# One fused attention, MoE and gated-MLP kernel on one core: the first group's x parts taken straight from PSUM, and one recombination started at another distance

## The chip, the cores and the metric

The kernel runs on one NeuronCore of one Trainium2 chip. The metric is the device time of one execution in microseconds; the median of several runs is compared. TensorE is called PE here, VectorE DVE, ScalarE ACT, GpSimd POOL and SyncE SP, as in the profile.

## What is computed

The reference chains three stages. Attention works within chunks of 64 tokens; its output becomes x, 2304 tokens by 512. A mixture of four experts (MoE) follows, then one gated layer with a clip (MoE2). All is float32.

```python
scores = scale * np.matmul(q_c, k_c.transpose(0, 1, 2, 4, 3))     # chunks of 64, 8 heads of 64
attn = softmax(scores); out = np.matmul(attn, v_c)
x = out.transpose(0, 2, 1, 3).reshape(B * S, H * D)               # 2304 x 512
for e in range(4):
    h = np.maximum(x @ w1[e], 0.0)                                # 512 -> 1024
    y += p[:, e:e + 1] * (h @ w2[e])                              # 1024 -> 512
h = y @ w_in                                                      # 512 -> 2048
g = h * np.clip(h + 3.0, 0.0, 6.0) / 6.0
return g @ w_out                                                  # 2048 -> 512
```

## The kernel before

**Arithmetic.** PE multiplies in a format with a shortened mantissa (fp32r). Each float32 operand is therefore split in a high part (a rounding copy) and a low part (what is left over), and each product is done in three: high by high, high by low, low by high (the list `HL`). Most large products also go through a scheme of the Strassen kind with seven products in place of eight (P1 to P7 for the first weight matrix, M1 to M7 for the second); its sums and differences run on DVE, ACT and POOL.

**Order of work.** The 2304 tokens make three sets of 768; a set's tokens lie in two halves of N = 384, even and odd tokens. Phase 0 is the MoE, phase 1 is MoE2; a unit is one set with one group of 512 hidden columns. `h_pair` (its products stand at L1003) computes h in seven products; `y_unit` (L1344), `y_sevens` (L1181), `y_turned` (L1240) and `y_turned_plain` (L1292) compute y. The very first group, that is phase 0, set 0, group 0, is done in plain products (`h_plain`, L1062) and in three units of 128 even and 128 odd tokens, so that PE can begin before all of the set's attention is done.

**The first set's attention** is six items, each of 256 tokens and four heads (two pairs of heads): items 0 and 1 are tokens 0 to 255, 2 and 3 the next 256, 4 and 5 the last. An item (`Item.place`) loads q and k, sorts even from odd tokens on ACT, DVE or POOL (L484), transposes both on PE (L494), copies them out of PSUM (L497), multiplies scores (L512), takes the maximum and subtracts it on DVE (L536, L556) and exponentiates on ACT (L560), or leaves the subtraction to ACT's bias (`on_act`, L544); sums and divides (L564 to L570); transposes the weights on PE (L574), copies them out (L577) and multiplies by v (L583). `end` then copies the result from PSUM to `xs` (L606), and `build_plain` makes the high part of x from `xs` on ACT (L761) and the low part on DVE (L764). The weights of the first group are split by `split_w` into a high part on ACT (L789) and a low part on DVE or POOL (L791).

**Who orders it.** All instructions are given to a planner (`Plan`): each has an engine, an estimated duration, a due time, buffers that it takes and buffers that it uses. The planner plays the program through with these estimates, picks on each engine the ready instruction with the earliest due time, and writes the instructions down in that order; on the chip each engine runs its own list in order and waits at semaphores. So a change of a due time or of an estimate can move any instruction. While PE would have nothing to do before 24 us, the planner puts in a filler: a matmul of the identity (L324), whose result nobody reads. Numbers at the head of the file (`ITEMS`, `LEAD`, `LOADS` and others) shift due times.

**PSUM** has eight banks under three names: four "h", three "y", one "a"; one "y" belongs to the filler while it is needed.

**MoE2's recombination.** For sets 0 and 1, `y_turned` adds the seven products of three groups into SBUF sums (L1251). Before the last group, `recombine_turned` turns them into the four quarters of the result with seven additions for each of two halves b (L1265): half 0 on POOL, half 1 on DVE, the latter due `RGAP` later. The gate of MoE2 is at L1094 (ACT), L1095 (DVE), L1117 (high part) and L1119 (low part); L1013 are the additions of the seven-product scheme behind h, L710 and L720 the high and low parts of x for the next set, L726 its differences.

## Time and profile before

| | |
|---|---|
| median of 3 runs | 1167.76 us (1167.74 to 1168.73) |
| the profiled execution, its time | 1167.89 us |
| the profiled execution, its span | 1166.0 us |
| PE busy | 1156.4 us, 99% |
| DVE, ACT, POOL busy | 751.2, 493.0, 537.0 us (64%, 42%, 46%) |
| chain that ended last, by engine | PE 97%, DVE 2%, the rest 1% |
| HBM traffic | 220.76 MB read, 83.36 MB written, 261 GB/s over the span |

The span runs from the first to the last instruction of the core. PE is busy nearly all of it, so the three other engines matter where PE waits for them, and the first 60 us, in which the attention of the first set is made, are read by themselves.

### The profile page before, as it was taken

How to read it: one execution, taken by the hardware profiler on the slowest of the kernel's cores; microseconds unless marked ns; L12 is line 12 of the kernel's file. 1: busy time of each engine (PE TensorE's matmuls, PEld its weight loads, DVE VectorE, ACT ScalarE, POOL GpSimd, SP SyncE). 2: the span in 40 equal slices, each digit the busy share in tenths (PEclk: the TensorE clock that was granted, in tenths of full speed). 3: DMA queues.
4: the chain of work that ended last, by engine and by line, in shares of the span. 5: the costliest groups of instructions: out<-in, count | busy, mean ns of one | idle time of the engine just before them, and what ended most of it. 6: DMA issues, size and time to landing. Idle time of an engine off the chain costs nothing.

```text
span 1166.0 us, 20404 instructions
## 1 busy us (share of the span) xinstructions
PE 1156.4 (99%) x7286; PEld 1070.7 (92%) x7286; DVE 751.2 (64%) x1473; ACT 493.0 (42%) x1182; POOL 537.0 (46%) x464
## 2 busy tenths in 40 slices
PE   8999999999999999999999999999999999999998
PEld 8899888889999988889999998999999999999997
DVE  5656555558756656569646556568479947884685
ACT  6754444535253343425342333233533454435432
POOL 3577655665341252536442534343445244614470
PEclk9999999999999999999999999999999999999999
DMA  9579888767869989874878787987795789669751
GB/s 243 221 255 335 287 299 273 265 239 233 250 214 309 319 299 299 280 269 134 269 291 306 266 296 251 308 345 263 283 302 198 201 333 292 211 197 353 253 182 55
DMA packets 175910, 305.49 MB, mean 262 GB/s; under 512 B 95168, under 2 KB 101568, under 8 KB 175808
## 3 DMA queue, kind: packets, MB, share of 16 engines
q1 hardware_dynamic: 174064, 302.48, 76.5%
q10 hardware_dynamic: 1744, 1.70, 0.4%
q8 instruction: 58, 0.95, 0.3%
q14 instruction: 44, 0.36, 0.1%
HBM read 220.76 MB, written 83.36 MB: 261 GB/s over the span
## 4 chain that ended last, share of the span: by engine, by line
PE 97%; DVE 2%; issue 1%; ACT 0%; POOL 0%; DVEq 0%; POOLq 0%; ACTq 0%
PE h L1003 43%; PE y L1344 35%; PE y L1240 4%; PE h L1240 2%; PE y L1181 2%; PE y L1292 2%; PE h L1062 2%; PE h L1181 1%; PE a L1240 1%; PE h L1292 1%; PE a L574 1%; PE a L1181 1%; PE y L324 1%; PE h L583 0%; PE y L494 0%
## 5 line engine op out<-in xcount | busy, mean ns | idle before, releaser
L1003 PE MATMUL h<-x,wh 128*128 128x384 f32 x2940 | 520.0, 335 | 1.6 <-DVE t L1095 1.6
L1003 PEld LDWEIGHTS h<-x,wh 128*128 128x128 f32 x2940 | 510.1, 188 | 4.9 <-DVE t L1095 2.6
L1344 PE MATMUL y<-wy,gt 128*128 128x512 f32 x1800 | 421.7, 392 | 0.1
L1344 PEld LDWEIGHTS y<-wy,gt 128*128 128x128 f32 x1800 | 335.0, 188 | 70.2 <-DVE acc L1381 1.4
L1381 DVE SCALAR_TENSOR_TENSOR acc<-y,pn,acc 128x512 f32<-128x512 f32 x126 | 89.0, 749 | 135.0 <-PE y L1344 135.0
L1086 ACT ACTIVATE gt<-h 128x384 fp32r<-128x384 f32 (+1 forms) x150 | 69.1, 489 | 115.7 <-DVE h L1013 114.7
L1013 DVE TENSOR_TENSOR h<-h,c 128x384 f32<-128x384 f32 x152 | 85.2, 563 | 35.4 <-PE h L1003 34.7
L1119 POOL TENSOR_TENSOR gt<-t,gt 128x384 fp32r<-128x384 f32 x54 | 54.5, 1016 | 114.3 <-ACT gt L1117 113.7
L939 POOL TENSOR_TENSOR w<-w,rh 128x512 f32<-128x512 f32 x28 | 37.6, 1343 | 137.1 <-DVE rh L936 83.2
L1020 ACT COPY p<-h 128x384 f32<-128x384 f32 x70 | 33.6, 480 | 152.8 <-PE h L1003 152.7
L1013 DVE TENSOR_TENSOR c<-h,p 128x384 f32<-128x384 f32 x70 | 38.9, 556 | 82.4 <-PE h L1003 73.1
L1087 DVE SCALAR_TENSOR_TENSOR gt<-h,gt 128x384 fp32r<-128x384 f32 (+1 forms) x150 | 76.5, 541 | 21.7 <-ACT gt L1086 20.7
L791 POOL TENSOR_TENSOR wp<-t,wp 128x512 fp32r<-128x512 f32 x36 | 47.3, 1314 | 50.4 <-ACT wp L789 50.4
L1094 ACT ACTIVATE t<-h,half 128x384 f32<-128x384 f32 x84 | 46.1, 581 | 49.6 <-DVE h L1013 45.5
L791 POOL TENSOR_TENSOR wy<-t,wy 128x512 fp32r<-128x512 f32 x32 | 41.1, 1293 | 43.5 <-ACT wy L789 43.5
L791 POOL TENSOR_TENSOR wp<-rh,wp 128x512 fp32r<-128x512 f32 x24 | 31.2, 1298 | 61.5 <-ACT wp L789 38.4
L1013 DVE TENSOR_TENSOR c<-h,c 128x384 f32<-128x384 f32 x70 | 38.8, 554 | 18.2 <-PE h L1003 17.6
L720 POOL TENSOR_TENSOR x<-xs,x 128x384 fp32r<-128x384 f32 x16 | 18.5, 1170 | 67.4 <-ACT x L710 67.3
L1117 ACT CAST gt<-t 128x384 fp32r<-128x384 f32 x66 | 33.0, 516 | 27.6 <-POOL t L1126 19.1
L710 ACT CAST x<-xs 128x768 fp32r<-128x768 f32 x33 | 27.1, 835 | 40.9 <-DVE xs L726 33.4
L791 POOL TENSOR_TENSOR wh<-t,wh 128x512 fp32r<-128x512 f32 x28 | 36.9, 1333 | 13.7 <-ACT wh L789 13.7
L789 ACT CAST wp<-t 128x512 fp32r<-128x512 f32 x36 | 22.6, 629 | 41.1 <-DMA k<-wp 18.5
(266 smaller groups left out, 1590.1 us busy)
## 6 DMA issues: line engine op xcount, KB each, us to landing
wh<-k SPq DMA_DIRECT2D x182, 512.0 KB, 6.2
wy<-k SPq DMA_DIRECT2D x104, 512.0 KB, 5.4
k<-wp SPq DMA_DIRECT2D x60, 512.0 KB, 5.2
k<-wh SPq DMA_DIRECT2D x49, 512.0 KB, 4.4
k<-wy SPq DMA_DIRECT2D x32, 512.0 KB, 4.5
wp<-k SPq DMA_DIRECT2D x18, 512.0 KB, 6.5
t<-in_moe_w_dram SPq DMA_DIRECT2D x32, 256.0 KB, 4.9
rh<-in_moe_w_dram SPq DMA_DIRECT2D x8, 1024.0 KB, 7.7
```

Of the source, the lines that this page charges most:

```text
L791: return op(eng, gps(512) if eng == "POOL" else dve(512), lambda: e.tensor_tensor(out=view(b.t[:, 1]), in0=read(), in1=raw(view(b.t[:, 0]) ...
L939: nc.gpsimd.tensor_tensor(out=low(), in0=low(), in1=dst(), op=ALU.mult)
L1003: nc.tensor.matmul(acc.t[:, :n], W.t[:, a, k_ * 256 + pr_ * P:k_ * 256 + (pr_ + 1) * P], X.t[:, b, k_, cs], start=new and first, stop=last ...
L1013: add = lambda out, x, y: (lambda: nc.vector.tensor_tensor(out=out(), in0=x(), in1=y(), op=ALU.add))
L1086: hi = op("ACT", act(n), lambda: nc.scalar.activation(hi_(), src(), AF.Relu), due, after, [G], bufs)
L1087: lo = op("DVE", dve(n), lambda: nc.vector.scalar_tensor_tensor(out=lo_(), in0=src(), scalar=0.0, in1=raw(hi_()), op0=ALU.max, op1=ALU.sub ...
L1094: x = op("ACT", act(n), lambda: nc.scalar.activation(r_(), src(), AF.Relu, bias=half, scale=1.0 / 6.0), due, after, [R], bufs)
L1119: lo = op(eng, dve(N) if eng == "DVE" else gps(N), lambda: e.tensor_tensor(out=where()[:, 1], in0=r_(), in1=raw(where()[:, 0]), op=ALU.sub ...
L1181: nc.tensor.matmul(ps[j].t[:, 256 * i:256 * i + 256], Gs[k][2]()[:, a, j * P:(j + 1) * P], part(b)[:, 256 * k:256 * k + 256], start=k == 0 ...
L1240: nc.tensor.matmul(ps.t[:, :N], part(c)[:, 256 * k + b * P:256 * k + (b + 1) * P], Gs[k][2]()[:, a], start=k == 0 and n == 0, stop=k == 1 ...
L1344: nc.tensor.matmul(ps[j].t, G.t[:, a, o + j * P:o + (j + 1) * P], W.t[:, b, :], start=f == FO[0] and i == 0, stop=f == FO[-1] and i == len ...
L1381: fn = lambda: nc.vector.scalar_tensor_tensor(out=A.t, in0=ps.t, scalar=p, in1=A.t, op0=ALU.mult, op1=ALU.add)
```

## The change

The line numbers of the new file are higher by 11 at the items (L494 becomes L505), by 52 to 54 at the products and gates (L1003 becomes L1055, L1095 becomes L1149, L1265 becomes L1319).

1. `end_plain` takes the place of `end` and `build_plain` for the first set. For each of the two PSUM banks of values, ACT rounds the high part from PSUM straight into the operand (`high`, L629), DVE subtracts it from PSUM into the low part (`low`, L633), and the copy to `xs`, which later groups need, is made by ACT after that (due `COPY` later).
2. `h_plain` has a new argument `parts_`. The first unit's products over the first two slices of 128 inputs are now in two passes: first for all four outputs those with x's high part, then those with its low part. The third pass, over the other two slices, is as before.
3. For each item, tables now name the engine of the sorts (`SORT_ON`), of the copies out of PSUM (`LEAVE_ON`) and of the division (`WEIGH_ON`), whether ACT takes the bias (`ON_ACT`), its PSUM banks, and a shift of the due time of each of its steps (`TURN`).
4. In `recombine_turned` DVE's half is due `T_GAP` = 3.0 after POOL's, where it was `RGAP` = 6.98; `RGAP`, now 0.13, is left for the third set's `recombine`.
5. Nearly all numbers that shift due times have other values, and so have the planner's estimates for fillers and for DVE beside POOL. The computation is the same.

```diff
-EARLY = 12.99
-RGAP = 6.98
-VLOADS = (4.01, 6.0, 12.0)
+EARLY = 7.02
+RGAP = 0.13
+T_GAP = 3.0
+T_ON = ("POOL", "DVE")
+VLOADS = (4.05, 6.0, 13.63)
+SORT_ON = (('ACT', 'DVE'), ('DVE', 'ACT'), ('ACT', 'ACT'), ('ACT', 'ACT'), ('ACT', 'ACT'), ('DVE', 'POOL'))
+WEIGH_ON = ('DVE', 'DVE', 'POOL', 'POOL', 'DVE', 'POOL')
+LEAVE_ON = (('ACT', 'ACT'), ('ACT', 'DVE'), ('ACT', 'ACT'), ('DVE', 'DVE'), ('ACT', 'DVE'), ('ACT', 'ACT'))
+ON_ACT = (0, 0, 0, 1, 0, 1)
+COPY = (3.0, 3.0, -0.77, 0.0, 0.0, 0.0)
...
-    EVERY = 0.6
-    DENSE = 7.7
+    EVERY = 1.53
+    FILL = 0.56
+    DENSE = -3.55
...
-    SHARED = 0.87
-    YIELD = 0.06
+    SHARED = 1.19
+    YIELD = 0.29
...
+        def high(self, c):
+            for s_, hi, _ in self.halves(c):
+                nc.scalar.copy(hi, s_)
+
+        def low(self, c):
+            for s_, hi, lo in self.halves(c):
+                nc.vector.tensor_tensor(out=lo, in0=s_, in1=raw(hi), op=ALU.subtract)
...
+        def end_plain(self, due, then, later):
+
+            x = op("PE", self.nu * 0.18, self.values, due, *self.values_need(), side=True)
...
+            for c in range(2):
+                his.append(op("ACT", n * act(self.nu * CH // n), lambda c=c: self.high(c), then, [x], () if c else new, [self.px[c], *bs]))
+                los.append(op("DVE", n * dve(self.nu * CH // n), lambda c=c: self.low(c), then, [his[c]], (), [self.px[c], *bs]))
...
+            self.last = [op("ACT", 0.34 if n > 1 else act(self.nu * CH), lambda c=c: self.leave(c), then + later, [x], (), [self.xs, self.px[c]]) for c in range(2)]
+            return self.last
...
-    def h_plain(u, f, zs, ks, acc):
+    def h_plain(u, f, zs, ks, acc, parts_=(0, 1)):
...
                 for i, (a, b) in enumerate(HL):
+                    if b not in parts_:
+                        continue
...
-                recombine_turned(si, b, t + 14 * one - soon(u) + RGAP * b, ("POOL", "DVE")[b])
+                recombine_turned(si, b, t + 14 * one - soon(u) + T_GAP * b, T_ON[b])
...
-            after = it.end(t + 8.0)
-            build_plain((0, 0), 128 * i, 128, after, t + 9, (m,))
-            first_set += after
+        after = it.end_plain(t + 8.0 + turn[11], t + 9 + turn[12], COPY[x])
+        first_set += after
...
-                firsts = [h_plain(u, f, (0, 1), range(2), None) for f in range(GF)]
+                firsts = [None] * GF
+                for ks in (ps for i, ps in PARTS if not i and ps[-1] < 3):
+                    for part in range(2):
+                        firsts = [h_plain(u, f, (0, 1), ks, firsts[f], (part,)) for f in range(GF)]
```

Three places in the order of the instructions follow. The first is PE from its first instruction. `ident` is the identity, `t` the sorted k and then q of item 0, `w_242` the sorted q and `w_244` the sorted k of item 1, `h` the banks of item 0's scores. Before:

```order
L324 MATMUL y<-ident 128x128 x11
L494 MATMUL y<-ident,t 128x128 x4
L324 MATMUL y<-ident 128x128 x2
L494 MATMUL y<-ident,t 128x4x32 x4
L324 MATMUL y<-ident 128x128
L494 MATMUL y<-ident,w_242 128x4x32 x4
L512 MATMUL h<-tri 64x64 x16
```

and now:

```order
L335 MATMUL y<-ident 128x128 x5
L505 MATMUL y<-ident,t 128x128 x4
L335 MATMUL y<-ident 128x128
L505 MATMUL y<-ident,t 128x4x32 x4
L505 MATMUL y<-ident,w_242 128x4x32 x4
L523 MATMUL h<-tri 64x64 x16
```

Six of the eleven fillers ahead of the first transposes are gone, and two of the three among the transposes. In all there are 12 fillers where there were 28.

The second is ACT ahead of item 3's exponentials (the row with x8). Before, in the rows from the high part of x for item 1 (`x_65<-xs`) on, where `wy<-t` rounds second weights and `tri<-a` copies item 2's transposed weights out:

```order
L761 CAST x_65<-xs 128x2x2x128
L789 CAST wy<-t 128x512
L577 COPY tri<-a 128x512
L789 CAST wy<-t 128x512 x3
L544 ACTIVATE e,st<-y,st 128x64 x8
L1086 ACTIVATE gt<-h 128x256 x4
```

and now, from item 1's copies to `xs` on, where `t<-kr` is the sort of k of item 4 and `gt<-h` are gates of the first unit:

```order
L617 COPY xs<-y 128x2x2x32 x2
L841 CAST wy<-t 128x512 x3
L1140 ACTIVATE gt<-h 128x256
L588 COPY tri<-a 128x512
L841 CAST wy<-t 128x512
L495 COPY t<-kr 128x512
L1140 ACTIVATE gt<-h 128x256
L555 ACTIVATE e,st<-y,st 128x64 x8
```

Two gates and a sort now stand ahead of the exponentials, where the four gates stood behind them and the sort was POOL's.

The third is DVE while it recombines set 0 (the rows of set 1 read alike). `c<-h,p`, `c<-h,c` and `h<-h,c` or `y<-h,c` are the additions behind h, `t<-t,h` the gates. Before:

```order
L1265 TENSOR_TENSOR kr<-acc,kr 128x384
L1095 SCALAR_TENSOR_TENSOR t<-t,h 128x384 x2
L1013 TENSOR_TENSOR y<-h,c 128x384
L1119 TENSOR_TENSOR gt<-t,gt 128x384 x2
L1095 SCALAR_TENSOR_TENSOR t<-t,y 128x384
L1013 TENSOR_TENSOR h<-h,c 128x384
L720 TENSOR_TENSOR x_65<-xs,x_65 128x384
L1119 TENSOR_TENSOR gt<-t,gt 128x384
L1095 SCALAR_TENSOR_TENSOR t<-t,h 128x384
```

and now:

```order
L1065 TENSOR_TENSOR c<-h,p_9987 128x384
L1319 TENSOR_TENSOR vr<-tri,acc 128x384
L1065 TENSOR_TENSOR c<-h,c 128x384
L1319 TENSOR_TENSOR tri<-tri,acc 128x384
L1319 TENSOR_TENSOR acc<-acc 128x384
L1065 TENSOR_TENSOR h<-h,c 128x384
L1319 TENSOR_TENSOR kr<-acc,kr 128x384
L1149 SCALAR_TENSOR_TENSOR t<-t,h 128x384 x2
L1065 TENSOR_TENSOR y<-h,c 128x384
L1065 TENSOR_TENSOR h<-h,c 128x384
L1173 TENSOR_TENSOR gt<-t,gt 128x384 x2
L1149 SCALAR_TENSOR_TENSOR t<-t,y 128x384
```

The row after the last shown is `L1149 ... t<-t,h`: the last addition behind h and the last gate now stand ahead of the next x (L769, which was L720). The step `vr<-tri,acc`, which stood ahead of `c<-h,p`, now stands behind it.

## Rows read from the trace of the kernel before

**Rows 1.** The page, busy time of each engine over the span.
```profile
PE 1156.4 (99%) x7286; PEld 1070.7 (92%) x7286; DVE 751.2 (64%) x1473; ACT 493.0 (42%) x1182; POOL 537.0 (46%) x464
```

**Rows 2.** PE's waits over the span: line, who was waited for: us in total, times, longest.
```profile
PE h L1003 <- DVE t L1095: 1.6, 2, 0.8
PE h L574 <- DVE e L570: 1.5, 2, 0.9
PE y L324 <- POOL ident masks.py:199: 1.4, 1, 1.4
PE y L512 <- ACT wp L497: 0.5, 1, 0.5
PE y L494 <- ACT tri L497: 0.4, 1, 0.4
```

**Rows 3.** The chain of waits, 0 to 70 us: start us, us, what.
```profile
1.36 5.06 PE y L324 x22
6.42 0.71 PE y L494 x4
7.14 0.45 PE y L324 x4
7.58 0.44 PE y L494 x4
...
8.70 0.71 PE h L512 x32
...
21.02 0.71 PE h L1062 x6
...
30.61 0.71 PE y L1344 x3
...
41.09 2.87 PE h L1062 x24
```

**Rows 4.** Two windows: us; PE, PEld, DVE, ACT, POOL busy; PE clock; DMA share, GB/s.
```profile
0.00:5.00 5.00, 3.64 (x17) 3.64 (x18) 0.33 (x4) 1.90 (x2) 0.70 (x6) 1.00 0.58 164
...
20.00:25.00 5.00, 5.00 (x97) 4.56 (x95) 2.16 (x5) 4.40 (x12) 1.61 (x2) 1.00 1.14 236
```

**Rows 5.** Timeline of PE: start us, us, line, operation, shapes, [idle before, releaser].
```profile
14.96 0.66 PE L574 MATMUL h<-ident,e 128*128 128x128 f32 x4 [0.63 <-DVE e L570]
...
16.82 0.69 PE L583 MATMUL h<-tri,vr 64*64 64x64 f32 x32
```

**Rows 6.** Timeline of ACT, same columns.
```profile
4.35 0.62 ACT L484 COPY t<-qr 128x512 f32<-128x512 f32 x1
...
17.56 0.77 ACT L606 COPY xs<-h 128x128 f32<-128x128 f32 x4 [0.79 <-PE h L583]
...
24.94 1.66 ACT L789 CAST wy<-t 128x512 fp32r<-128x512 f32 x3
...
29.14 0.34 ACT L544 ACTIVATE e<-y,st 128x64 f32<-128x64 f32 x1
```

**Rows 7.** Timeline of DVE, same columns.
```profile
4.79 0.43 DVE L484 COPY t<-kr 128x512 f32<-128x512 f32 x1 [3.86 <-DMA kr<-in_k_dram]
...
10.70 0.75 DVE L556 TENSOR_TENSOR e<-h,st 128x256 f32<-128x256 f32 x2
11.36 1.29 DVE L791 TENSOR_TENSOR wh<-rh,wh 128x512 fp32r<-128x512 f32 x2
...
14.22 0.68 DVE L570 TENSOR_TENSOR e<-e,st 128x512 f32<-128x512 f32 x1
```

**Rows 8.** Timeline of DVE around the first long wait of PE.
```profile
892.62 1.41 DVE L1265 TENSOR_TENSOR tri<-tri,acc 128x384 f32<-128x384 f32 x1
...
895.71 0.54 DVE L1265 TENSOR_TENSOR kr<-acc,kr 128x384 f32<-128x384 f32 x1
...
899.78 0.56 DVE L720 TENSOR_TENSOR x<-xs,x 128x384 fp32r<-128x384 f32 x1
...
900.71 0.56 DVE L1095 SCALAR_TENSOR_TENSOR t<-t,h 128x384 f32<-128x384 f32 x1
```

**Rows 9.** Timeline of PE there.
```profile
901.32 2.87 PE L1003 MATMUL h<-x,wh 128*128 128x384 f32 x15 [0.79 <-DVE t L1095]
```

**Rows 10.** Timeline of POOL there: its last step of the recombination.
```profile
893.57 1.33 POOL L1265 TENSOR_TENSOR qr<-acc,qr 128x384 f32<-128x384 f32 x1
```

More of the change, by code (lines that the diff above doesn't have):

```diff
@@ L187, in fill @@
             nonlocal seq
-            us = 0.45 if now < self.DENSE else 0.23
+            us = self.FILL if now < self.DENSE else 0.23
             o = Op("PE", us, self.filler, 0.0)
@@ L606, in leave, with halves, place @@
                     nc.scalar.copy(d[:, i], src[:, i])
[L608 removed]
+        def halves(self, c):
+            w, m0, ks = self.nu * CH, self.c0 // P, slice(self.ps[0] % 2, self.ps[-1] % 2 + 1)
+            src = self.px[c].t[:, :w].rearrange("p (i m z q) -> p i m z q", m=self.nm, z=2, q=Q)
+            to = [xx[self.ps[0] // 2][:, :, i, ks].rearrange("p z k (m c q) -> p c k m z q", c=2, q=Q)[:, c, :, m0:m0 + self.nm] for i in range(2)]
+            for i in range(len(self.ps)):
+                yield src[:, i], to[0][:, i], to[1][:, i]
+        def high(self, c):
[4 more added lines that the diff above has]
+                nc.vector.tensor_tensor(out=lo, in0=s_, in1=raw(hi), op=ALU.subtract)
+        def place(self, t, step, banks="asaas", loads=(), leave_on=("ACT", "ACT"), on_act=True, weigh_on="POOL", queues=("SP", "SP"), s_hold=0.0, sort_on=("ACT", "DVE"), before=None, turn=(0.0,) * 14):
             o = {}
@@ L768, in build_plain @@
             for z_ in range(2)[z]:
-                xplain[key[1], c0, d, z_] = los
+                for k in range(2)[ks]:
+                    xplain[key[1], c0, 2 * d + k, z_] = [hi], los
     xplain = {}
@@ L783, in keep, with split_w @@
         stored[ph, g, name] = op("SP", 0.5, lambda: nc.sync.dma_start(out=raw(D), in_=raw(b.t)), due, after, (), [b], lag=1.35, slack=KEPT, hold=hold)
-    def split_w(b, src, after, due, new, use, halves=True, hold=0.0, eng="POOL"):
+    def split_w(b, src, after, due, new, use, halves=True, hold=0.0, eng="POOL", then=0.0):
         read = src or (lambda: raw(b.t[:, 1]))
@@ L790, in split_w @@
         e = nc.gpsimd if eng == "POOL" else nc.vector
-        return op(eng, gps(512) if eng == "POOL" else dve(512), lambda: e.tensor_tensor(out=view(b.t[:, 1]), in0=read(), in1=raw(view(b.t[:, 0])), op=ALU.subtract), due, [hi, *after], (), [b, *use], hold=hold, pair=True)
+        return op(eng, gps(512) if eng == "POOL" else dve(512), lambda: e.tensor_tensor(out=view(b.t[:, 1]), in0=read(), in1=raw(view(b.t[:, 0])), op=ALU.subtract), due + then, [hi, *after], (), [b, *use], hold=hold, pair=True)
     def load_h(ph, g, due, hold):
```

128 lines of the change are left out of this document (73 added, 55 removed).

## The prediction

> **What bounds the kernel now.** I read the busy times first. TensorE (PE) works 1156.4 of 1166.0 us [rows 1], so what a change can win is PE's idle time, and time that PE fills with work nobody needs. The page cannot tell these apart, so next come PE's waits: the two long ones in mid-kernel are 1.6 us together, PE's products at L1003 waiting for VectorE (DVE) at L1095; those for the first group's softmax, DVE at L570, are 1.5 us; the rest of the list belongs to the first 20 us too [rows 2]. Then the chain of waits over the first 60 us: it begins with 22 passes of the filler matmul, 5.06 us, and until the first real product at 21.02 PE does little else than fill and wait [rows 3]. From there it is nearly dense: L1344 begins at 30.61, the second unit of products at 41.09. Last, the timelines of the three engines that feed PE at the start [rows 5 to 7], and the stretch around the first of the two long waits [rows 8 to 10].
>
> So there are two places: the start, to about 41 us, and the two stops at 900 and 1020 us. Between them no wait of PE is listed, and the same products stand there in both kernels, so I cost the other shifted numbers at nothing: PE's queue of products covers them. If a weight or an operand came late, that cover would be gone and PE would stop as at 900 us, about 0.8 us a time.
>
> **The start, step by step.** PE at first works at the lower of its two levels: a filler pass takes 5.06/22 = 0.23 us; from 7.14 on it takes 0.45/4 = 0.11 us [rows 3]. [...]
>
> (a) Fillers. 11 become 5 ahead of the first transposes. They end at 1.36 + 10 x 0.23 = 3.7, so PE stands idle until DVE has sorted k of item 0, at 4.79 + 0.43 = 5.2 [rows 7]; before, k's transposes waited for the fillers until 6.42. Four transposes at 0.23, a filler at 0.46 and q's four, the level rising under them as before, end at about 7.2. ScalarE (ACT) sorted q by 4.97 and copies the result out in 0.6 [rows 6], so item 0's scores start at 7.95 instead of 8.70 [rows 3]: 0.75 earlier.
>
> (b) DVE. Ahead of item 0's division (L570, 14.22) DVE now also copies k of item 1 out (0.6, as ACT's copy-outs) and does the fourth weight split (1.29/2 = 0.65) [rows 7]: 14.22 - 0.75 + 1.25 = 14.7, and 0.1 for ACT's part of the splits.
>
> (c) PSUM. The weights' transpose (L574) now goes to the bank "a" that held item 1's scores, so it must follow their two subtractions (0.75) as well as the division (0.68): 14.8 + 0.65 + 0.75 = 16.2 instead of 14.96 [rows 5]. One copy (0.7) and a handover later, at 17.55 instead of 16.82, come item 0's values.
>
> (d) x's parts. Before, four copies (0.77), a rounding and DVE's subtraction stand between values and products. Now four roundings straight from PSUM, nearest row the four copies of the same shape, 0.77 [rows 6]; the copies to xs (another 0.77) stand behind. DVE's one subtraction of 512 columns (0.65, as a weight split's) becomes four of 128; each costs between a quarter of that and one 256-column step (0.75/2 = 0.38), so 0.65 to 1.5 together; I take 0.85, nearest to the split, which is the same operation. They are off the path, as PE has 16 products of the high part first. High part ready: 17.55 + 0.7 + 0.77 = 19.0; PE meanwhile does item 2's scores (0.7) and item 1's transpose, so the first product comes at 19.4 instead of 21.02, 1.6 earlier. Ten more products are ready at once there, and I count 1.8 us ahead when PE is through with the first unit's products.
>
> (e) What is late next. ACT's eight exponentials of item 3 end before at 29.5 [rows 6]. Now they stand behind three weight roundings (1.66), a fourth, a sort moved from GpSimd (POOL) and two gates; they end at about 29.7. Item 4's transposes wait for the "y" bank that these exponentials read, and L1344 stands behind the transposes on PE and behind DVE's copy (0.6): it starts at 30.7, as before (30.61), with one transpose group (0.44) more done. So of 1.8 us some 0.35 are left; at the second unit's products (41.09) I count 0.65, since fillers and short gaps after 31 us also go. Bounds: 0.1 if the queue costs 0.25 more, 1.8 if ACT keeps up. I take **0.65**, nearest to L1344's row.
>
> (f) Moved transfers and sorts. SP now sends q of item 3 ahead of v, so v lands one load of 256 KB later; before, the values of 16.82 waited for the copy, not for v. POOL loses seven of its eight sorts; PE's waits of rows 2 are not for these.
>
> **The two stops.** Before, DVE runs its half of the recombination (L1265) beside POOL's: 1.41 us for a step that takes 0.54 once POOL is done [rows 8, 10]. Then the L1095 that frees the bank PE wants comes behind a subtraction for the next x (L720, 899.78) and one more step, at 900.71, and PE starts again at 901.32 after 0.79 us idle [rows 8, 9]. In the new order one recombination step moves behind the first sum, costing some 0.3, but L1013 and then L1095 no longer stand behind these two (900.71 - 899.78 = 0.93): PE's release moves from 901.3 to about 900.6, and the stop to almost nothing. ACT's queue follows the same order. Twice: **1.5 us**; bounds 0.4 (a slow step more each) to 1.6 (all idle time). The third set's recombination moves by one place; PE has no gap there and I give it nothing.
>
> **Sum.** The profiled execution took 1167.89 us, 0.13 above the median of 1167.76. 1167.89 - 0.65 - 1.5 = 1165.74, less 0.13: **1165.6 us**. A measurement of this kernel can tell about 0.2% (2.3 us) from no change, so faster means below 1165.4: the forecast lies at the edge.
>
> [...] PE reached the upper level after matmul fillers, 1.36 to 6.42 [rows 3]; the change keeps 5 of these 11. [...]
>
> **The rivals.**
> - *Nothing is lost behind the exponentials* (0.2). ACT's order is as told, but if its pieces start a little sooner, or the level is up at once and scores come another 0.8 earlier, the 1.8 us of (d) stay: 1167.76 - 1.8 - 1.5 = 1164.4. For it: (a) to (d) rest on measured pieces; against: from 20 to 25 us ACT is busy 4.40 of 5 us already [rows 4].
> - *The level rises one step later* (0.13), after item 1's transposes. Scores then run at the lower level and start 0.35 later, end about 1.05 later: 1166.7. For it: PE's idle 1.5 us before 5.2.
> - *The recombination does not do what it says* (0.06): POOL's and DVE's steps still collide and the stops stay at 0.7: 1166.9.
> - *Slower: the clock* (0.17). If the upper level is not there when the first product comes at 19.4, because PE had idle time and transposes where it had fillers, the chain pays 1.05 up to the scores, then a second 0.45 for each of the two transposes and 0.7 each for values and item 2's scores (2.3), and the products run at half speed as long as fillers did before the rise, 5.5 us, losing 2.75: 1165.6 + 6.1 = 1171.7. Of this, 4.5 decide: above 1170.1 it counts as slower. For it: between 11 and 19 us PE now works on little. Against: before, too, PE idled up to 0.9 us at a time there [rows 2], and passes stayed at 0.11.
>
> **How the numbers follow.** Forecast 0.44, its own range 1164.6 to 1166.6: half of it below 1165.4. Faster: 0.22 + 0.20 = 0.42. Same: 0.22 + 0.13 + 0.06 = 0.41. Slower: 0.17. The range takes in the first three rivals with the bounds of their terms and a partial loss of the clock; it leaves out the last rival (0.17) and 0.03 at the low end: 1162.8 to 1169.0.
>
> **What would show it.** Right: no filler row of 22 passes; first product near 19.4; L1344 first near 30.7; PE's wait for L1095 gone from the list; PE's idle time down by some 1.5 us after 60 us. Wrong: transposes at 0.23 us a pass after 8 us (clock); a new wait of PE in the list of waits between 60 and 1160 us; a first product later than 21; L1344 clearly before 30 (then ACT was faster than I have it, and the gain near 3.3).

## The result, and the profile after

| | before | changed |
|---|---|---|
| median | 1168.24 us (8 runs, 1167.74 to 1168.81) | 1174.99 us (8 runs, 1171.40 to 1178.60) |
| ratio, 95% interval | | 1.0058 (1.0047 to 1.0068) |
| profiled execution | 1167.89 us | 1178.60 us |
| start of the first L1003 / L1055 | 66.03 us | 69.86 us |
| end of the last product | 1162.18 us | 1172.97 us |

The changed kernel is slower by 0.58%, 6.8 us, outside the range of 1162.8 to 1169.0. Its own runs lie 7 us apart where those of before lie 1 us apart, and the profiled one is the longest of them. In that execution 10.8 us are lost up to the last product: 3.8 of them before the second group's products begin (L1003 before, L1055 now), the rest in the middle.

PE's busy time and its waits (as in [rows 1, 2]; engine, tile, line, releaser: us in all, times, longest):

```profile
PE 1160.1 (99%) x7254; PEld 1072.3 (91%) x7254; DVE 747.6 (64%) x1496; ACT 494.3 (42%) x1203; POOL 524.6 (45%) x456
```

```profile
PE h L594 <- DVE gt L1141: 4.1, 1, 4.1
PE a L585 <- DVE e L567: 1.6, 1, 1.6
PE y L505 <- DVE t L495: 1.6, 1, 1.6
PE y L505 <- ACT wh L495: 1.5, 1, 1.5
...
PE y L505 <- ACT e L555: 1.1, 1, 1.1
PE h L523 <- DVE gt L1141: 0.7, 1, 0.7
```

The wait for L1095 (now L1149) is gone, as forecast: the two stops of 900 and 1020 us are no longer there. Two things are new. One wait of 4.1 us stands alone, at 413.76, where before had none. And PE is 3.7 us busier than before [rows 1] with the same products. Part of that is products at the lower level, as a table of stretches shows (start and end, length, busy time of PE, PEld, DVE, ACT, POOL, granted clock, DMA share, GB/s; [rows 4] are the same view of before):

```profile
5.00:10.00 5.00, 4.52 (x48) 4.07 (x49) 1.02 (x3) 2.86 (x7) 0.00 (x0) 1.00 1.11 364
10.00:15.00 5.00, 3.46 (x48) 3.03 (x48) 4.71 (x10) 4.18 (x9) 0.00 (x0) 0.97 1.26 282
15.00:20.00 5.00, 3.37 (x16) 2.88 (x15) 4.73 (x13) 1.60 (x4) 0.00 (x0) 0.50 1.05 292
20.00:25.00 5.00, 5.00 (x118) 4.73 (x118) 2.70 (x10) 3.44 (x12) 0.00 (x0) 0.85 1.25 218
415.00:420.00 5.00, 1.44 (x28) 1.08 (x30) 2.64 (x6) 4.31 (x12) 2.54 (x2) 0.75 1.06 366
420.00:425.00 5.00, 5.00 (x35) 4.03 (x36) 1.49 (x6) 2.32 (x16) 0.64 (x1) 0.57 1.05 388
```

The column's 1.00 from 5 to 10 us does not agree with the times of the passes, as it did not from 0 to 5 us before [rows 3, 4], and I go by the passes: four transposes take 1.12 us at 5.48 and 1.11 at 9.73, then 0.72 at 11.06 (PE's timeline), and the level is up only from 11.3 on (before: 6.9). PE then works 3.46 and 3.37 us of 5, and the level is low again from 14.7 to 21.6 us (granted clock 0.50 from 15 to 20; four transposes take 1.09 us at 17.70, and 0.66 at 21.77), a stretch that holds the transpose of item 0's weights and item 0's values; the first product follows at 22.18. The granted clock is 0.50 a second time behind the stop at 414, from 417.5 to 424.3.

The chain of waits over the start (start, us, what):

```profile
5.48 1.12 PE y L505 x4
...
8.73 1.06 PE h L523 x32
...
12.23 2.40 DVE wh L843 x4
...
16.29 0.60 DVE e L581
...
17.70 1.09 PE a L585 x4
...
22.42 1.92 PE h L1116 x16
...
28.20 0.64 PE y L523 x32
...
30.89 1.92 ACT e L555 x13
```

Each of the forecast's times is passed late: the division 16.3 for 14.7, the weights' transpose 17.7 for 16.2, the first product 22.4 for 19.4; L1398 (L1344 before) begins at 34.56 for 30.7.

The stop of 4.1 us, in the engines' timelines (start, us, engine, line, operation, idle time ahead of it and what ended it): POOL, SP's queue, ACT, DVE and PE, in this order.

```profile
395.81 1.30 POOL L843 TENSOR_TENSOR wp<-rh,wp 128x512 fp32r<-128x512 f32 x1
```

```profile
405.44 1.65 SPq L970 DMA_DIRECT2D w<-in_moe_w_in_dram  x1
407.19 0.38 SPq L932 DMA_DIRECT2D wy<-k  x1
407.66 0.38 SPq L835 DMA_DIRECT2D k<-wp  x1
```

```profile
407.08 0.47 ACT L1072 COPY p<-h 128x384 f32<-128x384 f32 x1
415.13 0.62 ACT L841 CAST wp<-t 128x512 fp32r<-128x512 f32 x1 [7.57 <-DMA k<-wp]
415.65 0.66 ACT L973 ACTIVATE t<-w 128x512 f32<-128x512 f32 x1
416.21 0.66 ACT L976 ACTIVATE w<-w 128x512 f32<-128x512 uint32 x1
416.76 0.85 ACT L1140 ACTIVATE gt<-h 128x384 fp32r<-128x384 f32 x2
```

```profile
417.27 1.02 DVE L1141 SCALAR_TENSOR_TENSOR gt<-h,gt 128x384 fp32r<-128x384 f32 x2 [7.36 <-ACT gt L1140]
```

```profile
417.88 1.38 PE L594 MATMUL h<-tri,vr 64*64 64x64 f32 x24 [4.12 <-DVE gt L1141]
```

ACT is to round a weight of MoE2 (L841) into one of two "wp" buffers; the buffer is free only when its store (L835) has landed. POOL had the buffer ready at 397.1; the store was issued 10.6 us later, at 407.66, behind loads in SP's queue, and landed at 415.1. In ACT's queue the conversions (L973, L976) and the gates (L1140) stand behind that rounding, DVE's L1141 behind the gates, and the "h" bank that PE wants behind that. Between 410 and 415 us DVE, ACT and POOL do nothing at all (columns as in the table of stretches):

```profile
410.00:415.00 5.00, 3.76 (x20) 3.15 (x18) 0.00 (x0) 0.00 (x0) 0.00 (x0) 1.00 0.97 370
```

### The profile page after: what moved, and what is told of

Same layout as the page of the kernel before. It is cut to its first block, busy times and chain, and to the rows that moved or that the text cites. A ratio compares the mean times of both kernels' runs of the same rounds, so it can differ in the third digit from the quotient of the medians.

```text
span 1176.8 us, 20404 instructions
## 1 busy us (share of the span) xinstructions
PE 1160.1 (99%) x7254; PEld 1072.3 (91%) x7254; DVE 747.6 (64%) x1496; ACT 494.3 (42%) x1203; POOL 524.6 (45%) x456
## 4 chain that ended last, share of the span: by engine, by line
PE 95%; DVE 2%; DMA 1%; issue 1%; ACT 1%; POOL 1%; SPq 0%; DVEq 0%; ACTq 0%; POOLq 0%
PE h L1055 42%; PE y L1398 34%; PE y L1294 4%; PE h L1294 2%; PE y L1235 2%; PE y L1346 2%; PE h L1235 1%; PE h L1116 1%; PE a L1294 1%; PE h L1346 1%; PE a L585 1%; DMA k<-wp 1%; PE a L1235 1%; PE y L505 0%; PE h L523 0%
## 5 line engine op out<-in xcount | busy, mean ns | idle before, releaser
L1055 PE MATMUL h<-x,wh 128*128 128x384 f32 x2940 | 521.5, 335 | 0.0
L1055 PEld LDWEIGHTS h<-x,wh 128*128 128x128 f32 x2940 | 510.0, 188 | 4.1 <-DVE c L1065 1.1
L1398 PE MATMUL y<-wy,gt 128*128 128x512 f32 x1800 | 422.8, 393 | 0.5 <-DVE tri L508 0.3
L1398 PEld LDWEIGHTS y<-wy,gt 128*128 128x128 f32 x1800 | 336.5, 188 | 71.1 <-DVE acc L1435 0.9
L1435 DVE SCALAR_TENSOR_TENSOR acc<-y,pn,acc 128x512 f32<-128x512 f32 x126 | 88.9, 749 | 132.4 <-PE y L1398 132.2
L1140 ACT ACTIVATE gt<-h 128x384 fp32r<-128x384 f32 (+1 forms) x150 | 68.7, 487 | 105.7 <-DVE h L1065 104.1
L1065 DVE TENSOR_TENSOR h<-h,c 128x384 f32<-128x384 f32 x152 | 85.1, 562 | 32.3 <-PE h L1055 30.8
L1141 DVE SCALAR_TENSOR_TENSOR gt<-h,gt 128x384 fp32r<-128x384 f32 (+1 forms) x150 | 76.5, 540 | 32.3 <-ACT gt L1140 31.1
L769 POOL TENSOR_TENSOR x<-xs,x 128x384 fp32r<-128x384 f32 x16 | 17.0, 1092 | 88.4 <-ACT x L759 58.7
L581 POOL TENSOR_TENSOR e<-e,st 128x384 f32<-128x384 f32 (+1 forms) x19 | 16.4, 863 | 80.8 <-DVE st L563 48.4
L841 ACT CAST wp<-t 128x512 fp32r<-128x512 f32 x36 | 22.2, 621 | 66.6 <-DMA k<-wp 30.8
L1171 ACT CAST gt<-t 128x384 fp32r<-128x384 f32 x66 | 32.6, 516 | 27.0 <-POOL t L1180 19.4
```

What stands on the lines that cost most here:

```text
L1055: nc.tensor.matmul(acc.t[:, :n], W.t[:, a, k_ * 256 + pr_ * P:k_ * 256 + (pr_ + 1) * P], X.t[:, b, k_, cs], start=new and first, stop=last ...
L1065: add = lambda out, x, y: (lambda: nc.vector.tensor_tensor(out=out(), in0=x(), in1=y(), op=ALU.add))
L1140: hi = op("ACT", act(n), lambda: nc.scalar.activation(hi_(), src(), AF.Relu), due, after, [G], bufs)
L1141: lo = op("DVE", dve(n), lambda: nc.vector.scalar_tensor_tensor(out=lo_(), in0=src(), scalar=0.0, in1=raw(hi_()), op0=ALU.max, op1=ALU.sub ...
L1398: nc.tensor.matmul(ps[j].t, G.t[:, a, o + j * P:o + (j + 1) * P], W.t[:, b, :], start=f == FO[0] and i == 0, stop=f == FO[-1] and i == len ...
L1435: fn = lambda: nc.vector.scalar_tensor_tensor(out=A.t, in0=ps.t, scalar=p, in1=A.t, op0=ALU.mult, op1=ALU.add)
```

## The experiments

Theory A: the loss has two parts, the clock at the start, and the rounding near 414 us with the clock behind it; rival C, that the first group's new order is late by itself, was taken into it as a third part after the first four runs. In these kernels the planner's order is kept and only what the diff says is inserted or moved (`MORE`: extra fillers ahead of an instruction, by the planner's number; `MOVE`: another place in the written order). 14 is the transpose of item 0's k, 82 a transpose of item 3, 22 and 24 the weights' transpose and the values of item 0.

### The start

```diff
 class Plan:
+    MORE = {14: 4}                       # e1_start_fill
+    MORE = {82: 6, 22: 7, 24: 2}         # e2_thin_fill
+    MORE = {14: 4, 82: 6, 22: 7, 24: 2}  # e3_both_fill
...
-            o.fn()
+            [self.filler() for _ in range(self.MORE.get(o.n, 0))], o.fn()
```

**e1.** 

> The changed kernel with four more fillers ahead of the first transposes, so that PE works without the gap of 1.62 us at 3.86; nothing else is moved. Theory A (the start is lost to the clock, and the clock to the missing fillers at the beginning and, apart from that, in the thin stretch from 11 to 18 us): the granted clock rises near 6.9 us as before instead of 11.3, scores start at about 8.0, but PE works as little as before from 11 to 18 us, so the clock falls there again: the first product comes between 21.0 and 22.2, L1398 at 33.5 to 34.5, and the time falls by 0 to 1.5 us against the changed kernel. Rival B (only the late rise matters): the clock holds to the end, first product near 20, L1398 near 31, time down by 3 to 4 us. Rival C (the new order of the first group is late by itself, DVE's extra work and the bank a): the clock is full and the first product still comes at 21 or later with L1398 at 33 or later.

**e2.** 

> The changed kernel with fifteen more fillers in the thin stretch alone: six ahead of the transposes of 14.60, seven ahead of the weights' transpose of 17.70, two ahead of item 0's values. The start is as in the changed kernel, so the clock rises at about 11.3. Theory A: the clock then stays at full through 14.7 to 21.5, first product at 20.3 to 21.0, L1398 at 31 to 32.5, time down by 2 to 3.5 us against the changed kernel. Rival B (only the late rise matters): the clock falls all the same, and the fillers, twice as long then, push the first product to 23 or later. Rival C (the order is late by itself): clock full, L1398 still at 33.5 or later, time down by under 1 us.

**e3.** 

> Both sets of fillers in the changed kernel. Theory A: the clock rises near 6.9 and stays, first product at 19.4 to 20.3 (the forecast of the prediction), L1398 at 30 to 31.5, time down by 3.5 to 4.5 us against the changed kernel; what is left over the kernel before is then the stop of PE near 414 us and the clock behind it. Rival C: L1398 at 33 or later with the clock full, time down by under 1.5 us.

| | level up | low again, up to 60 us | first product (PE's timeline) | L1398 | L1055 | median, us (runs) |
|---|---|---|---|---|---|---|
| changed | 11.3 | 14.7 to 21.6 | 22.18 | 34.56 | 69.86 | 1174.99 (8) |
| e1 | 4.4 | 14.7 to 21.5 | 20.80 | 33.45 | 68.76 | 1171.52 (6) |
| e2 | 10.7 | no | 20.74 | 33.36 | 68.65 | 1172.48 (5) |
| e3 | 6.3 | no | 19.38 | 32.01 | 67.30 | 1170.26 (12) |

e1, the stretches in which it falls again (columns as above):

```profile
10.00:15.00 5.00, 2.04 (x42) 1.59 (x38) 4.91 (x12) 3.30 (x7) 0.00 (x0) 0.96 1.25 281
15.00:20.00 5.00, 4.18 (x74) 3.90 (x74) 3.26 (x10) 2.51 (x7) 0.00 (x0) 0.50 0.94 273
```

So both sets of fillers are needed, each gives nearly half, and together they are worth 69.86 - 67.30 = 2.56 us. The rival that only the late rise matters falls with e1. But rival C has a part too: in e2 and e3 L1398 comes 0.9 and 0.5 us later than the latest that theory A allowed, and with the clock up from 6.3 us on, L1055 still begins 1.27 us later than before. The same first 60 us stand in e5, e11, e13 and e14, where L1055 begins between 67.08 and 67.50, so this loss is 1.05 to 1.47 us. e3's own rows show where it arises (chain of waits):

```profile
14.80 0.60 DVE e L581
...
16.21 0.63 PE a L585 x4
...
19.63 1.46 PE h L1116 x10
...
22.49 0.75 ACT x L629 x4
...
24.36 0.86 PE h L1116 x5
...
25.66 0.64 PE y L523 x32
...
28.34 1.92 ACT e L555 x13
30.28 0.53 ACT e L555 x3
...
32.01 0.96 PE y L1398 x3
```

Up to the first product this is the forecast: 19.6 in this view, in which 19.4 was forecast and before had 21.02 [rows 3]. Then item 3's scores come at 25.66 (before 24.42), its exponentials at 28.34 (before 27.09), and L1398 3.67 us behind these. Ahead of the scores stand, in this chain, the high part of item 1's x (22.49), its low part on DVE (23.62) and five products that use it (24.36). In PE's own order 30 of the first unit's 48 products (16, 8 and 6) now come before item 3's scores, where 18 (6 and 12) did before.

The medians of e1 to e3 fall further than the start explains; the stops near 414 us differ from one kernel's profile to the next (1.7, 1.2 and 2.3 us between 412 and 416). In e3 the clock is also low behind that stop, from 415.9 to 419.4 us (mean 0.66 from 415 to 420), and its profile has one more stop, of 1.60 us, which ends at 386.69. It is of the same kind: ACT's conversion L973 waits for a load, DVE's steps of that conversion (L979 to L988) wait for ACT, and behind them in DVE's queue stands the sum L1435 that PE wants.

```profile
382.34 0.66 ACT L973 ACTIVATE t<-w 128x512 f32<-128x512 f32 x1 [5.71 <-DMA w<-in_moe_w_out_dram]
```

**e10.** The bank, on e3, with two fillers fewer ahead of the weights' transpose:

```diff
-    MORE = {14: 4, 82: 6, 22: 7, 24: 2}
+    MORE = {14: 4, 82: 6, 22: 5, 24: 2}
...
-BANKS = ('hhahh', 'yahay', 'ayaay', 'yyyyy', 'ayaay', 'ayaay')
+BANKS = ('hhhhh', 'yahay', 'ayaay', 'yyyyy', 'ayaay', 'ayaay')
```

> The changed kernel with both sets of fillers (two fewer ahead of the weights' transpose) and with the bank of item 0's weights' transpose as before: h in place of a; the order of instructions is otherwise that of the run with both fillers. The prediction's term (c) put 0.75 us on that bank (two subtractions of item 1). If it lies on the path to the end of the first group, the transpose begins at 15.3 to 15.8 us instead of 16.2, the first product at 18.6 to 19.0 instead of 19.38, and the products of the second weight set 0.4 to 0.8 us earlier than 67.30. Rival (ScalarE's queue and GpSimd's division set the pace behind the first product): under 0.2 us there.

PE's timeline, and ACT's row of item 3's first exponential:

```profile
14.88 0.66 PE L585 MATMUL h<-ident,e 128*128 128x128 f32 x4 [0.23 <-DVE e L581]
...
18.50 2.14 PE L1116 MATMUL h<-x,wh 128*128 128x256 f32 x16
...
29.42 0.66 PE L505 MATMUL y<-ident,t 128*128 128x128 f32 x4 [1.14 <-ACT e L555]
...
30.87 0.50 PE L1398 MATMUL y<-wy,gt 128*128 128x512 f32 x1 [0.35 <-DVE tri L508]
```

```profile
27.19 0.32 ACT L555 ACTIVATE e<-y,st 128x64 f32<-128x64 f32 x1 [0.69 <-DVE st L551]
```

L1055 at 66.16, 1.14 us earlier than e3: the bank was on the path to the end of the first group. Not all of the 1.14 us is the bank's. e16 (below) has the same instructions up to 60 us; its level rose at 6.75 us (e10: 5.1), its first product came at 19.19 and L1055 at 66.85, 0.52 us earlier than in e5, which differs from it in the bank and these two fillers alone. So the bank is worth 0.5 to 1.1 us, which takes in the 0.75 put on it.

The first product is now 2.3 us earlier than before (18.50 for 20.78, PE's timeline) and L1055 0.1 us later. PE works on almost without a gap from there, but 12 more products (1.7 us), item 3's second transposes (0.4) and a filler (0.2) now stand between the first product and item 3's scores and take the lead up: the scores begin at 24.43, before at 24.35, and the exponentials where they did before (27.09), although ACT was free for 0.69 us ahead of them. Median 1169.48.

**e7, e8.** The kernel before without some fillers, nothing else moved:

```diff
-            o.fn()
+            o.fn() if not (o.n < 0 and 2.9 < o.start < 5.5) else None   # e7_before_few
+            o.fn() if not (o.n < 0 and 9.0 < o.start < 21.0) else None  # e8_before_thin
```

> The kernel before with five fillers in place of eleven ahead of its first transposes, every other instruction as before. Theory A (the late rise costs the clock at the start, the thin stretch keeps it only where it has fillers): the clock rises between 7 and 11.5 us, not at 6.9, and stays, since the fillers from 9 to 21 us are still there; the products of the second weight set begin 0.3 to 1.5 us later than at 66.03. Rival (the fillers at the beginning are not needed): rise by 7 us and the time within 0.3 us of before or up to 0.7 us less, as k's transposes start earlier.

> The kernel before with its first eleven fillers kept and those between 9 and 21 us left out, every other instruction as before. Theory A: the clock rises at about 6.9 and falls again in the thin stretch between 12 and 18 us, for some us; the products of the second weight set begin 1 to 3 us later than at 66.03. Rival (once risen it holds through PE's work there, as the denser scores and transposes of the kernel before are enough): within 0.3 us of before.

e7: level up at 9.1 and no fall (granted clock 1.00 in each stretch up to 25 us); L1003 at 66.96, 0.93 us later; median 1169.40. e8: low from 13.3 to 23.5, L1003 at 68.05, 2.0 us later; median 1169.06. So the kernel before, too, has a low level there without the fillers of 9 to 21 us. In these stretches its granted clock is 1.00 with them (the first two rows; [rows 4] for 20 to 25 us), and in e8 0.83, 0.50 and 0.65 (the other three):

```profile
10.00:15.00 5.00, 3.54 (x55) 2.88 (x54) 4.93 (x13) 3.57 (x7) 1.76 (x3) 1.00 1.26 280
15.00:20.00 5.00, 4.08 (x85) 3.54 (x86) 4.29 (x12) 2.66 (x8) 0.38 (x1) 1.00 0.91 258
```

```profile
10.00:15.00 5.00, 1.93 (x40) 1.39 (x40) 4.93 (x12) 3.26 (x7) 1.67 (x3) 0.83 1.25 280
15.00:20.00 5.00, 3.23 (x69) 2.74 (x70) 3.84 (x11) 2.51 (x7) 0.44 (x1) 0.50 1.14 315
20.00:25.00 5.00, 5.00 (x55) 4.80 (x55) 1.98 (x5) 2.87 (x8) 1.04 (x1) 0.65 1.18 216
```

### The stop near 414 us

**e4.** 609 to 614 are two weight roundings with their subtractions and stores, 635 and 636 the conversion L973, L976:

```diff
 class Plan:
+    MOVE = {609: 414.98, 610: 415.7, 611: 417.3, 612: 416.62, 613: 417.4, 614: 418.8, 635: 412.2, 636: 412.3}
...
-        for o in sorted(self.ops, key=lambda o: (o.start, o.n)):
+        for o in sorted(self.ops, key=lambda o: (self.MOVE.get(o.n, o.start), o.n)):
```

> The changed kernel with ScalarE's weight rounding of the staging that waited for a store (L841, 407 to 415 us, with its subtraction, its store and the next one) issued behind the gates and the copies of values that stood behind it; nothing else is moved. Theory A (the gates only stood behind that rounding in ScalarE's queue): PE's stop of 4.1 us near 414 falls to 0.5 us or less, the clock stays at full there, and the time falls by 4 us (the stop alone) to 7.5 us (with the clock of 417 to 424) against the changed kernel in a run like the profiled one. Rival D (the gates were late for something else, as the additions on DVE or the weights): the stop stays at 2 us or more. Rival E (the stop is there in some executions alone): the median falls by under 2 us.

PE's 4.1 us are gone; after 60 us the longest stop is 0.47 us, and the clock does not fall near 414 (the execution's mean granted clock is 0.998, which its low stretch at the start makes up; the changed kernel's is 0.994). The start is as late as the changed kernel's (L1055 at 69.73), yet the last product ends at 1165.57, 7.4 us earlier. Median 1171.45, 3.5 us less: the stop is not of the profiled length in every execution. The runs spread over 2.2 us here, over 7.2 in the changed kernel. Theory A holds, rival D falls.

**e5, e16.** e3 and e4 together, and both with e10's bank:

```diff
+    MOVE = {609: 414.98, 610: 415.7, 611: 417.3, 612: 416.62, 613: 417.4, 614: 418.8, 635: 412.2, 636: 412.3}
+    MORE = {14: 4, 82: 6, 22: 7, 24: 2}   # e5_all; e16_repaired: 22: 5, and BANKS as in e10
```

> The changed kernel with both sets of fillers and with ScalarE's rounding behind the gates: the two losses that the first four runs showed taken away together. Theory A (three separate costs: the clock of the start 2.6 us, the stop near 414 us with its clock, and 1.3 us that the first group's new order costs even at full clock; against them 1.6 us from the recombination): the products of the second weight set begin at 67.3 us as with the fillers alone, no stop of over 0.5 us after 60 us, and the median is 1167.8 to 1169.2 us, within 0.1% of the kernel before, with a spread of under 2 us. Rival: other stops between 270 and 450 us take the place of the one removed, and the median stays above 1170.

> The changed kernel with everything that the runs found wrong mended and nothing else moved: both sets of fillers, the bank h for item 0's weights' transpose, ScalarE's rounding behind the gates near 407 us. By the sum of the single runs: 1169.3 (fillers and rounding) less 1.14 (bank) = 1168.2 us, the products of the second weight set at 66.2 us, no stop of over 0.5 us after 60 us, so no faster than the kernel before although the two stops of 900 and 1020 us are gone: some 1.5 us lie in short waits that the shifted numbers of mid-kernel make. If the costs are not additive (a stop comes back with the earlier start), the median is 1169 us or more.

e5: 1169.30 us (1167.95 to 1171.20, 11 runs), 0.1 us above theory A's range and with 3.3 us of spread, L1055 at 67.37. e16: 1168.79 us (1166.81 to 1170.30, 11 runs), ratio to before 1.0003 (0.9994 to 1.0012), L1055 at 66.85. The costs mostly add up, but both keep short stops between 431 and 443 us (1.2 and 1.6 us together), and e16 came 0.6 us above the sum, with L1055 0.65 us later than the sum had it, so the rival is half right. With all mended the change is worth nothing that these runs can tell from zero.

**e11, e13, e14.** e3 with numbers of before put back:

```diff
-STAGES = (-15.64, -46.32)
+STAGES = (8.32, -111.16)               # e13_stages, e11_mid_numbers
-LEAD = (15.49, 24.46, 6.51, 23.29)
+LEAD = (14.87, 24.88, 6.51, 9.55)      # e14_lead, e11_mid_numbers
```

e11 also has ITEMS, LOAD, FIRST, KEPT and EARLY of before.

> The changed kernel with both sets of fillers and with the numbers that place loads, stores and staging behind the first group as before (ITEMS, STAGES, LEAD, LOAD, FIRST, KEPT, EARLY); the first 60 us and the recombination are those of the run with both fillers. Theory A (those numbers made the stops between 270 and 450 us): no stop of over 0.3 us there, the median falls from 1170.3 to 1167.2 to 1168.4 us (1168.05 + 1.27 - 1.6 = 1167.7), and the runs lie within 2 us of each other in place of 6. Rival (the later start or the new plan as such makes the stops): stops of 0.5 us or more stay between 270 and 450 us and the median stays above 1169.

> The changed kernel with both sets of fillers and with STAGES alone as before (8.32, -111.16): when the weights of MoE2 are converted and split. Theory F (the stop near 414 us is a conversion's rounding that the new STAGES puts where PE's gates are short and the DMA queue is full): no stop of over 0.5 us between 380 and 450 us, median 1168 to 1170 us. Rival G (LEAD: the weights of the second products are loaded 14 us earlier and hold the queue up, so that any store is late): the stops stay, 1 us or more in sum between 270 and 450 us, median about 1170.

> The same with LEAD alone as before (its last number 9.55 in place of 23.29). Rival G: no stop of over 0.5 us between 380 and 450 us, median 1168 to 1169.5 us. Theory F: the stops stay, 1 us or more in sum, and the runs still spread over 3 us or more.

None of the three stops by over 0.05 us between 300 and 500 us, and the runs lie within 1.4, 2.4 and 1.5 us of each other (e3: 6.3). So the stop needs the new values of both numbers; that staging then falls where the gates are short, and that the weights loaded early fill the queue, is the reading of theories F and G together and is not shown by itself. Neither F nor G is right alone. But the medians, 1172.75, 1171.59 and 1170.69, do not fall below e3's 1170.26, and the expectations of 1167 to 1170 were missed. Each plan has other short stops (0.26 to 0.61 us, at 539, 788 and 829 us among others), which do not account for it: in e11's profile PE's gaps after 60 us come to 2.7 us, in e3's to 4.0, and e11's clock does not fall (mean 1.0). Why these three are slower stays open.

### The recombination

**e6.** The distance alone, in the kernel before:

```diff
-RGAP = 6.98
+RGAP, T_GAP = 6.98, 3.0
...
-                recombine_turned(si, b, t + 14 * one - soon(u) + RGAP * b, ("POOL", "DVE")[b])
+                recombine_turned(si, b, t + 14 * one - soon(u) + T_GAP * b, ("POOL", "DVE")[b])
```

> The kernel before with the recombination's distance alone changed (3.0 in place of 6.98 for MoE2's turned recombination); nothing ahead of 890 us is moved. The prediction's term: the two stops of 0.79 and 0.81 us at 900 and 1020 us go, 1.4 to 1.6 us gained, 1166.3 to 1166.8 us. Rival (the gain in the changed kernel came from its other numbers): under 0.5 us, with stops of 0.5 us or more left.

1167.47 us against 1168.06: 0.6 us, with an interval that takes in no change (ratio 0.9995, 0.9986 to 1.0004), and two stops of 0.68 us. DVE's rows there (two steps in a row, each beside one of POOL's, ahead of the second sum, for which PE now waits):

```profile
893.38 1.41 DVE L1265 TENSOR_TENSOR tri<-tri,acc 128x384 f32<-128x384 f32 x1
894.71 1.37 DVE L1265 TENSOR_TENSOR acc<-acc 128x384 f32<-128x384 f32 x1
896.00 0.54 DVE L1013 TENSOR_TENSOR c<-h,c 128x384 f32<-128x384 f32 x1
```

So the number itself does not do it; the order that the changed kernel's plan came to does. Four kernels make pieces of that order in the kernel before, with `MOVE` (the first of the two places; the second is alike, 503 numbers on):

```diff
+    MOVE = {3794: 893.2, 3795: 893.87, 3803: 894.9, 3804: 895.5, 3805: 896.3}  # e9b_gates_only: sum and gate ahead of the next x
+    # e9_recomb_moved: with 3775: 890.6, 3776: 891.7 (two steps behind the sums)
+    # e12_order_full: e9b with 3921: 898.0, 3922: 898.8, 3923: 900.3 (x behind the next sums)
+    # e15_order_exact: e12 with 3801: 898.02, 3802: 898.9 (gate roundings behind the copy for the sum)
```

> The kernel before with the changed kernel's order at the two places of the recombination and nothing else: two of DVE's recombination steps (L1265) stand behind the first and the second sum (L1013) in place of ahead of them, and the sum and the gate (L1013, L1095, with ScalarE's L1094) that free the bank which PE wants stand ahead of the next x (L720). The first theory, which the run with the distance alone did not bear out in this form, now says that this order and not the distance itself takes the stops away: both under 0.2 us, 1.3 to 1.6 us gained, 1166.4 to 1166.8 us. Rival: GpSimd's and DVE's steps collide elsewhere, stops of 0.5 us or more stay.

> The same with the second half alone: the sum and the gate ahead of the next x, and the recombination steps as in the kernel before. The prediction's reason was that L1095 stood behind a subtraction for the next x and one more step (0.93 us): by that the stops of 0.79 and 0.81 us fall to under 0.2 us here too, and 1.2 to 1.6 us are gained. Rival: the recombination steps ahead of the sums are what makes the gate late, half or more of the stops stays, and under 0.8 us is gained.

> The kernel before, at the two places of the recombination alone: as in the run with the gates alone, and the next two sums (L1013) ahead of both subtractions for the next x (L720), with ScalarE's copy (L1020) ahead of its rounding of x (L710). Theory: what was left there, PE's waits of 0.36 and 0.38 us for a sum, came of these subtractions: both go, and the median is 0.5 to 0.8 us below that of the run with the gates alone, 1.6 to 1.8 us below the kernel before (1166.3 to 1166.6 us), so it beats both kernels. Rival: the wait only moves on to the next sum, and the gain stays at 1.0 to 1.2 us.

> The kernel before, with the changed kernel's order of DVE and ScalarE from the fourth sum on at the two places of the recombination: against the run before this one, ScalarE's copy (L1020) and rounding of x (L710) also stand ahead of the two gate roundings (L1117), and DVE's sum (L1013) ahead of L1119. There the sum that PE waited for began 12.4 us after the unit's first product; in the changed kernel it begins at 12.1 and PE does not wait. Theory: both waits go (under 0.1 us each), 1.3 to 1.6 us gained, 1166.3 to 1166.7 us, which beats both kernels. Rival: 0.2 us or more of wait is left at each place and the median is 1167.0 to 1167.8 us.

| | stops at the two places, us | median, us (before in the same runs) | ratio, 95% interval |
|---|---|---|---|
| e9 | 0.44, 0.45 | 1167.55 (1168.16) | 0.9991 (0.9982 to 1.0000) |
| e9b | 0.36, 0.38 | 1167.09 (1168.16) | 0.9990 (0.9981 to 0.9998) |
| e12 | 0.38, 0.38 | 1167.75 (1167.91) | 1.0000 (0.9991 to 1.0009) |
| e15 | 0.10, 0.09 | 1166.86 (1168.23) | 0.9990 (0.9981 to 0.9999) |

e9b shows that the prediction's reason was half of it: with L1095 ahead of L720 half the stop is left, now for the sum behind. Moving the two recombination steps as well (e9) leaves no less. e12's wait moved on as its rival said: the next sum stood behind L1119, which waited for ACT. That its median gained nothing is not explained by this; its profile has a stop of 0.26 us at 113 us, as e6's has, that the profiles of before and of e9b do not have. Only with the order of all of these does the wait go, as PE's list of e15 shows:

```profile
PE h L574 <- DVE e L570: 2.0, 2, 1.1
PE y L324 <- POOL ident masks.py:199: 1.4, 1, 1.4
PE y L512 <- ACT wp L497: 1.0, 1, 1.0
PE y L494 <- ACT tri L497: 0.4, 1, 0.4
```

e15 is 0.1% below the kernel before, with an interval that just leaves out no change, and 0.7% below the changed one. e9b has the same ratio: the stops tell the two apart, the times do not.

## Why the prediction was wrong

**The start, (a) to (d): right as long as the clock is there.** In e3 scores 0 begin at 7.82 (forecast 7.95), the division at 14.72 (14.7), the weights' transpose at 16.21 (16.2), the first product at 19.6 (19.4); the high parts take 0.77 us, the low ones 0.89 (0.85). In the changed kernel itself the step that failed is "the level rising under them as before": it rose at 11.3, fell at 14.7, and cost 2.56 us at the second group's products. Step (a) priced the fillers it took away at a gain, and the profiles of e7 and e8 show the price of such fillers in the kernel before: 0.93 us for six of the eleven at the beginning, 2.0 us for those of 9 to 21 us.

**(e): the wrong queue.** The end of this step was right: item 4's transposes wait for these exponentials (1.1 us), and L1398 for DVE's copy. The queue ahead was wrong. It held that item 3's exponentials "stand behind three weight roundings", a sort and two gates on ACT, and end at 29.7. With the clock up they end at 30.8, and ACT waits for them to be ready: 0.68 us in e3, 0.69 in e10. What they wait for is item 3's scores (25.66 for 24.42). These stand in PE's queue behind 12 more products than before and, in e3's chain of waits, behind item 1's high and low parts. (c)'s bank puts all of it 0.5 to 1.1 us later; that the rest comes of the two passes and of the new due times is argued from the order, and no run tries it. Where I took 0.65 us gained at the start, the order alone loses 1.27 in e3.

**"I cost the other shifted numbers at nothing."** This is the largest error: with either STAGES or LEAD of before the stop near 414 us is not there (e13, e14). The text names the way it fails (a late operand, "0.8 us a time"), and gives it no chance and no place in the range. It was one stop of 4.1 and one of 0.7 us, and behind it products at half speed: by the two rows of 415 to 425 us, 1.44 us busy at half speed (granted clock 0.50 from 417.5 on) and 5.00 us at 0.57, 0.72 + 2.15 = some 2.9 us are lost, an estimate. e4 bears both out: without them its last product ends 7.4 us earlier, though it has 0.6 us of gaps of its own. What I read was PE's list of waits in the kernel before; what decided was a store late in SP's queue, a buffer of which there are two, and what stands behind it in ACT's queue.

**The two stops: right in size, half right in cause.** Both are gone, 1.6 us, with 1.5 forecast. The reason given moves the gate; e9b shows that this alone leaves 0.74 us of waits, and e6 that the distance alone leaves 1.36 us.

**The sum of the profiled execution.** 3.83 (start) + 4.80 (stops at 414) + 2.9 (clock behind them) - 1.6 = 9.9 of 10.8 us. The rest, 0.9 us, is not idle time: all of PE's gaps after 60 us come to 4.94 us there, so 0.14 without the two stops (before: 1.69, 0.09 without its two). It lies in stretches that count as busy and stays open, as does the 1 us that e16 loses after 60 us outside PE's listed waits.

**The rivals.** The slower one was right about the fillers: with them back, in e3, the level is not low again up to 60 us, and 2.56 us come back; "between 11 and 19 us PE now works on little" was the right row to fear. It was priced at 6.1 us, from a product rate that stays halved for 5.5 us. No run shows that; in the changed kernel the clock came back at 21.6, before the first product at 22.18, so by itself it gives 1165.6 + 2.6 = 1168.2, not 1171.7. The argument against it, that before PE idled there too, did not count that before had fillers in between: without them, in e8, the granted clock is 0.50 from 15 to 20 us, where before has 1.00. The rise itself came later than the second rival had it: at 11.3, in the midst of a transpose, with 32 score products and four filler passes among the 16 transposes since 5.48 (PE's timeline). Nor was a late rise the whole of it: in e1 the level was up at 4.4 and low again from 14.7.

## What to carry to other kernels

When a change shifts planner numbers along with its real edit, price the shifted numbers by what they put next to what: for each in-order queue, list what stands behind an instruction that waits for a buffer, and how far behind its plan the DMA queue already runs. In both kernels here the granted clock from 15 to 20 us, where PE has gaps, was 1.00 with the fillers of that stretch (before, e2, e3) and 0.50 without them (e8, the changed kernel, e1): taking them away is to be priced by the clock of all that follows until the level is back, and a lead won on one engine is worth only what the next late chain leaves of it.

## What was not expected

- The level rose at different moments in kernels whose first 60 us hold the same instructions: 6.9 us in the profile of before, 4.3 in e6 and e9, 6.8 in e9b, though PE had worked without a gap from 1.36 to the rise in each. The first product moved little: 20.78, 20.45 (e9), 20.75 (e9b).
- The low stretch differs too. e4 has the changed kernel's instructions at the start, but its level was low from 17.5 to 20.9 us alone, not from 14.7 to 21.6, and L1055 came only 0.13 us earlier (69.73).
- In e1 the level was up at 4.4 us and low again from 14.7, with PE busy 2.04 us of the 5 from 10 to 15. In e14, with both sets of fillers, it was up at 4.3 and stayed up for as long as there were products (the execution's mean granted clock is 1.0).
- A store of 512 KB that waited its turn took 7.4 us from issue to landing (407.66 to 415.1), after 10.6 us in SP's queue, and with two buffers this became 4.1 us of PE. Whether a third buffer would have hidden it is not tested.
- The stop near 414 us has another length in each execution: 4.8, 1.7, 1.2 and 2.3 us in the profiles of the changed kernel, e1, e2 and e3, whose order there is the same. The spread of a kernel's runs is a hint of such a stop, not a proof: of the five kernels that have it four spread by 5 to 7 us, but e1's six runs by 1.4; the six variants without it spread by 1.4 to 3.5.
